# Retention and a gated FFN on one core: two batches side by side, 64 tokens at a time

## Chip, core and metric

The kernel runs on one NeuronCore of a Trainium2 chip. The metric is the time of one execution in microseconds (us) on the device. TensorE multiplies matrices into PSUM, VectorE (DVE) and ScalarE (ACT) work elementwise, GpSimd (POOL) takes a few small operations, and SyncE (SP) issues nearly all DMAs. Each engine runs its instructions in the order in which the program lists them.

## What is computed

There are 4 batches, 8 heads of width 64 and 768 tokens. The first half is a retention: per batch and head a state of 64 x 64 decays by a head's own factor and takes in one outer product per token. The second half is a feed-forward layer of width 1,024 with a convolution over three tokens inside its gate.

```python
for t in range(S):                                    # S = 768
    state = gamma * state + einsum('bhd,bhe->bhde', k[:, :, t], v[:, :, t])
    y[:, :, t] = scale * einsum('bhd,bhde->bhe', q[:, :, t], state)
x = y.transpose(0, 2, 1, 3).reshape(B, S, 512)
h = maximum(x @ w_in, 0)                              # w_in 512 x 1024
conv = sum(conv_w[k] * shifted(h, k - 1) for k in range(3))
out = (h * sigmoid(conv)) @ w_out                     # w_out 1024 x 512
```

Everything is float32. The three weight arrays arrive as 64-bit floating-point words seen as pairs of 32-bit integers, and the kernel itself makes from them float32 values, split into a high part and a low part.

## The kernel before

**Retention.** Time is cut into pieces of 64 tokens. Decay is taken out of the recurrence by scaling v with gamma^-t (`scale_v`) and the result with gamma^t (`decay`, with the table `gy_sb`). A *chunk* `n` is 128 tokens of one batch, two pieces `s`, so there are 24 chunks. For a piece, `mix(n, s)` issues three sorts of products of 64 x 64, all on line L456: the state's update (`ps_st`), the result from masked scores and from the carried state (`ps_y`), and the scores of the chunk that follows (`ps_s`). State and scores lie on the diagonal quarters of the array ("straight"), the result on the other two ("crossed"), and they are issued two and two. Before the next piece can be mixed, ScalarE copies the state from PSUM (`carry`, L484), and VectorE masks the scores (`masked`, L476) and scales v (L420; from chunk 17 on POOL does).

**From y to x.** `decay` (L489) writes a chunk's x, ScalarE copies it as high part into `xu` (`x_head`, L503), VectorE writes the rest as low part (`x_rest`, L509), and POOL copies edge columns between neighbouring units (`halo`, L519).

**Weights.** 16 pieces of 128 x 512, 8 of `w_in` and then 8 of `w_out`, are loaded and turned into float32 by one ScalarE and five VectorE operations (`w_abs` to `w_low`, L547 to L581). ScalarE writes the high half (`w_head`, L598). For the low half there are two ways: for the first `SUMMED` = 6 pieces TensorE adds up three products with unit matrices (`w_sum`, L606 to L608) and ScalarE copies the sum (`w_add`, L626); for the others VectorE subtracts and adds (`w_rest` L613, `w_add` L628). A ninth, tiny one is the convolution's weights.

**FFN.** A *unit* `u` is 256 tokens of one batch with an edge column on both sides (258 columns); there are 12. `mm1(u, f)` (L640) computes 128 of the 1,024 hidden columns in 12 matmuls (four slices of x, three products of high and low parts). It needs weight piece `f`, and the halo from the next chunk. Then come `relu` (L649), `conv_tap` (L656), two `conv_side` (L661) per `f`, and per pair `p` of them `gate` (L667), `gated` (L672), `g_head` (L677), `g_rest` (L682). `mm2(u, t, p)` (L696) is 6 matmuls of 512 columns for 128 tokens `t`, and `put` copies and stores.

**Order and buffers.** No engine chooses at run time. `list_tasks` lists all steps with an assumed duration, what they need and which buffers they take; `tensor_sequence` gives TensorE's wanted order, and `plan` places step after step by these durations, slacks (`SLACK`) and windows; the steps are emitted in the order of their planned starts. Where the plan sees TensorE wait early in the program it adds warm-up matmuls on a tile of zeros (`keep_warm`, L386). Retention buffers `rw` are three, weights and gated values share four `g`, hidden values and `w_out` share 31 `h`, and PSUM has one bank for scores, two for results, two for `mm1`, two for `mm2`.

Of the kernel before, what the change touches and what calls it, by code (L numbers as in the profile page):

```python
# [20 lines left out]
NC = S // P  # L21
# [3 lines left out]
U = NT * P  # L25
UH = U + 2
NU = S // U
N_CHUNKS, N_UNITS = B * NC, B * NU
CONV = 2 * NF
LAST = (N_UNITS - 1, NT - 1)  # L30

# [10 lines left out]
BUFS = {"rw": 3, "x": 5, "xu": 3, "g": 4, "m": 2, "es": 1, "h": 31, "cv": 3, "ps_s": 1, "ps_y": 2, "ps_m": 2, "ps_o": 2}  # L42
# [5 lines left out]
LATENCY, SAME = {DMA: 2600, PE: 250}, {DMA: 0, PE: 50}  # L48
OTHER = 60
FIRST = {PE: 4800.0, DVE: 1200.0, ACT: 2000.0, POOL: 700.0, DMA: 700.0}  # L50
WARM_UP = 8
WARM_NS = 216
# [4 lines left out]
SWITCH = 95  # L57
MIX = 950
USE = {"scores": 0.25, "mix": 0.5, "mm1": 0.98, "mm2": 0.98, "w_sum": 0.98}

ATT_FIRST, ATT_RATE = 5, 16.5

CONV_FIRST, CONV_RATE, CONV_LAG = 24, 10.5, 32
SUM_LEAD, SUM_LEAD_OUT = 14, 201
AHEAD = 10984
WINDOW = {PE: 85200, POOL: 98300, DMA: 97750, DVE: 150}
STAY = 26
PACE = 1.4

SLACK = {  # L70
    "x_rest": 38500, "halo": 23000, "w_in": 42000, "w_out": -7500, "mix": -1000, "carry": -8000,
    "masked": 6000, "make_gy": 59500, "x_head": 44500, "scores": 36000, "g_rest": 14000, "scale_v": 8500,
    "conv_w": 28500,
}

VECTOR_V, VECTOR_X, SUMMED = 17, 48, 6
# [3 lines left out]
        "g_rest", "halo"}  # L80

def has_state(n, s):
    return (n % NC, s) != (NC - 1, 1)


def list_tasks():
# [6 lines left out]
    for n in range(N_CHUNKS):  # L93
        b, c = divmod(n, NC)
        u = n // NT

        before = ("load", n - 1) if n > 1 else n and ("load_kv", 0)
        task(("load", n), DMA, 4 * P * D * H * (4 if n else 2) * BYTE, [before], take="rw")
        if n == 0:
            task(("load_kv", 0), DMA, 4 * P * D * H * 2 * BYTE, [("load", 0)])  # L100
        vector = n < VECTOR_V
        task(("scale_v", n), DVE if vector else POOL, 690 if vector else 1230, [("load", n) if n else ("load_kv", 0)])
        if n == 0:
            for s in range(2):
                task(("scores", 0, s), PE, 485, [("load", 0), s and ("scores", 0, 0)], take=None if s else "ps_s")
        task(("masked", n), DVE, 690, [("mix", n - 1, 1) if n else ("scores", 0, 1)], free="ps_s")
        for s in range(2):

            prev = (n, 0) if s else (n - 1, 1) if c else (n - 1, 0) if b else None
            after = [("scale_v", n), ("masked", n), prev and ("carry", *prev)]  # L110
            after += [("mix", n, 0) if s else n and ("mix", n - 1, 1)]
            after += [n + 1 < N_CHUNKS and ("load", n + 1)]
            take = None if s else "ps_y" if n + 1 == N_CHUNKS else ("ps_y", "ps_s")
            task(("mix", n, s), PE, MIX, after, take, "rw" if s else None)
            if has_state(n, s):
                task(("carry", n, s), ACT, 370, [("mix", n, s)])
        if n == 0:
            task(("load_gy",), DMA, 4 * P * NPAIR * P * BYTE)
        elif n < NC:
            task(("make_gy", c), ACT, 1300, [("load_gy",)])  # L120
        task(("decay", n), DVE, 690, [("mix", n, 1), ("make_gy", c) if c else ("load_gy",)], "x", "ps_y")
        if n % NT == 0:
            task(("x_tiles", u), POOL, 60, [u and ("x_tiles", u - 1)], take="xu")
        task(("x_head", n), ACT, 620, [("decay", n), ("x_tiles", u)])
        vector = n < VECTOR_X
        task(("x_rest", n), DVE if vector else POOL, 690 if vector else 1280, [("x_head", n)], free="x")
        if n % NT == NT - 1 and u % NU + 1 < NU:
            task(("halo", n, 1), POOL, 620, [("x_rest", n), ("x_tiles", u + 1)])
        if n % NT == 0 and u % NU > 0:
            task(("halo", n, -1), POOL, 620, [("x_rest", n), ("x_tiles", u - 1)])  # L130

    task(("load_eye",), DMA, 300)
    task(("eyes",), ACT, 500, [("load_eye",)])
    for i in range(CONV + 1):
        big = i < CONV
        ns = lambda t: t if big else 90
# [4 lines left out]
        task(("w_abs", i), ACT, 670 if big else 220, [("load_w", i)], take="m" if big else None)  # L141
        task(("w_clamp", i), DVE, ns(410), [("w_abs", i)])
        task(("w_shift", i), DVE, ns(410), [("w_clamp", i)])
        task(("w_sign", i), DVE, ns(680), [("w_shift", i)])
        task(("w_power", i), DVE, ns(410), [("w_sign", i)])
        task(("w_low", i), DVE, ns(680), [("w_power", i)], take="es" if big and i < SUMMED else None)
        if not big:
            task(("w_add", i), DVE, 90, [("w_low", i)])
            continue
        task(("w_head", i), ACT, 620, [("w_sign", i)], take="h" if i >= NF else None)  # L150
        if i < SUMMED:
            task(("w_sum", i), PE, 1500, [("w_head", i), ("w_low", i), ("eyes",)], take="ps_m", free=("g", "m", "es"))
            task(("w_add", i), ACT, 600, [("w_sum", i)], take="h" if i >= NF else None, free="ps_m")
        else:
            task(("w_rest", i), DVE, 690, [("w_head", i), ("w_power", i)])
            task(
                ("w_add", i), DVE, 690, [("w_low", i), ("w_rest", i)], take="h" if i >= NF else None, free=("g", "m")
            )

    for u in range(N_UNITS):  # L160
        x = [("x_tiles", u)] + [("x_rest", NT * u + t) for t in range(NT)]
        x += [u % NU and ("halo", NT * u - 1, 1), u % NU + 1 < NU and ("halo", NT * u + NT, -1)]
        for f in range(NF):
            before = (u, f - 1) if f else (u - 1, NF - 1) if u else None
            task(
                ("mm1", u, f), PE, 1452, [("w_add", f), before and ("mm1", *before)] + (x if f == 0 else []),
# [3 lines left out]
            task(("relu", u, f), ACT, 380, [("mm1", u, f)], take=None if odd else "h", free="ps_m")  # L170
            task(
                ("conv_tap", u, f), ACT, 490, [("relu", u, f), ("w_add", CONV), odd and ("conv_tap", u, f - 1)],
                take=None if odd else "cv",
            )
            task(("conv_side", u, f, 0), DVE, 450, [("conv_tap", u, f)])
            task(("conv_side", u, f, 2), DVE, 450, [("conv_side", u, f, 0)])
            if not odd:
                continue
            task(("gate", u, p), ACT, 640, [("conv_side", u, f - 1, 2), ("conv_side", u, f, 2)])
            task(("gated", u, p), DVE, 690, [("gate", u, p)], free="h")  # L180
# [3 lines left out]
                ("g_head", u, p), ACT, 630,  # L184
                [("gated", u, p), before and ("g_head", *before), u and not p and ("load_w", CONV - 1)], take="g",
            )
            task(("g_rest", u, p), DVE, 690, [("g_head", u, p)], free="cv")
        for t in range(NT):
            halves = 2 if (u, t) == LAST else 1
            for h in range(halves):  # L190
                for p in range(NF // 2):
# [4 lines left out]
                        ("mm2", u, t, p, h), PE, 1400 / halves, need,  # L196
                        take=None if p else "ps_o", free="g" if t == NT - 1 and h == halves - 1 else None,
                    )
                task(("put", u, t, h), ACT, 580 / halves, [("mm2", u, t, NF // 2 - 1, h)], free="ps_o")
# [3 lines left out]
def tensor_sequence(tasks):  # L203

    visits = [[("scores", 0, s) for s in range(2)]] + [[("mix", n, s)] for n in range(N_CHUNKS) for s in range(2)]
    parts = []
    for u in range(N_UNITS):
        for p in range(NF // 2):
            j = NF * u + 2 * p + 1
            step = max(j + CONV_LAG, CONV_FIRST + CONV_RATE * j // 10) + 5  # L210
            parts += [(step, ("mm2", u, t, p, 0)) for t in range(NT)]
    sequence, sums, done, step = [], [], 0, -1
    while step < N_UNITS * NF or parts:

        for i in range(NF) if step < 0 else ():
            late = [(i - SUM_LEAD, ("w_sum", i))] if i < SUMMED else []
            late += [(CONV_FIRST + i - SUM_LEAD_OUT, ("w_sum", NF + i))] if NF + i < SUMMED else []
            sums += late
        sums.sort()
        while sums and sums[0][0] <= step:  # L220
            sequence.append(sums.pop(0)[1])
        if 0 <= step < N_UNITS * NF:
            sequence.append(("mm1", step // NF, step % NF))
        goal = max(done, min(ATT_FIRST + int(ATT_RATE * (step + 1) / 10), len(visits)))
        sequence += [k for some in visits[done:goal] for k in some]
        done = goal
        if parts and parts[0][0] <= step:
            sequence.append(parts.pop(0)[1])
        step += 1

    sequence = [k for k in sequence if k[:3] != ("mm2", *LAST)]
    return sequence + [("mm2", *LAST, p, h) for h in range(2) for p in range(NF // 2)]

# [532 lines left out]
```

## Time and profile before

| | |
|---|---|
| median of 3 timed runs | 374.64 us (373.19 to 375.74) |
| span of the profiled execution, first to last instruction | 371.3 us; the timed median stands 3.3 us above it |
| TensorE busy | 363.0 us, 98%, clock 0.999 |
| VectorE, ScalarE, POOL busy | 255.9, 203.0 and 21.3 us |
| first `mm1`, first `mm2` | 33.39 and 140.02 us |
| moved by DMA | 40.96 MB, mean 110 GB/s |

Times inside the profile count from the span's start. A row of the timeline gives start, duration, engine, line, operation, tiles and number; what stands in brackets behind it is the idle time before and what ended it. Rows of the chain give start, duration and what ran. A duration reaches to the end of an operation's result, so consecutive operations of one engine may start closer together than their durations.

### The profile page before, as it was taken

The numbers are of one execution on the slowest core, as the hardware profiler recorded it, in microseconds if no ns is written. First come the engines' busy times: TensorE is split into PE (matmuls) and PEld (weight loads), VectorE is DVE, ScalarE is ACT, GpSimd is POOL, SyncE is SP. The second block draws the span as 40 slices with busy tenths as digits, with TensorE's granted clock in tenths as the row PEclk, the third lists the DMA queues.
The fourth block names the chain that finished last, engine by engine and source line by source line (L and its number), as shares of the span: only waits on it lengthen the run. The fifth ranks groups of instructions, "written<-read, shape, count | busy, mean of one in ns | idle before, by whom it ended". The sixth has DMA issues, their size and how long they took to land.

```text
span 371.3 us, 10906 instructions
## 1 busy us (share of the span) xinstructions
PE 363.0 (98%) x4787; PEld 317.3 (85%) x4787; DVE 255.9 (69%) x484; ACT 203.0 (55%) x444; POOL 21.3 (6%) x53
## 2 busy tenths in 40 slices
PE   8999999998999989999999999999999999999996
PEld 6768778997999978889898998999899989888886
DVE  1588688898778867687657566575655555889860
ACT  3844554765444534556456456564545545678741
POOL 1001000010001121300000002010000000000000
PEclk9999999999999999999999999999999999999999
DMA  8877687406556657301000010000100001001111
GB/s 272 324 282 293 237 284 244 163 2 201 199 181 229 224 190 266 120 4 56 2 25 34 2 56 1 30 28 2 56 2 28 30 0 59 28 29 56 58 56 56
DMA packets 10047, 40.96 MB, mean 110 GB/s; under 512 B 1264, under 2 KB 1648, under 8 KB 7056
## 3 DMA queue, kind: packets, MB, share of 16 engines
q1 hardware_dynamic: 9936, 40.20, 29.6%
q8 instruction: 37, 0.61, 0.6%
q14 instruction: 10, 0.08, 0.1%
q0 software_dynamic: 64, 0.07, 0.1%
HBM read 33.98 MB, written 6.29 MB: 108 GB/s over the span
## 4 chain that ended last, share of the span: by engine, by line
PE 93%; ACT 4%; DMA 1%; issue 1%; SPq 0%; ACTq 0%
PE ps_m L640 38%; PE ps_o L696 36%; PE ps_st L456 6%; PE ps_s L456 5%; PE ps_y L456 3%; PE ps_o L386 3%; PE ps_m L606 2%; ACT gy_sb L416 2%; DMA gy_sb<-in_gy 1%; ACT cv L656 1%; PE ps_m L607 0%; PE ps_m L608 0%; ACT L667 0%; ACT L416 0%; ACT h L649 0%
## 5 line engine op out<-in xcount | busy, mean ns | idle before, releaser
L640 PE MATMUL ps_m<-xu,wi_hi 128*128 128x258 f32 x768 | 145.6, 287 | 1.4 <-issue 1.3
L696 PE MATMUL ps_o<-h,g 128*128 128x512 f32 (+1 forms) x600 | 143.7, 386 | 0.0
L640 PEld LDWEIGHTS ps_m<-xu,wi_hi 128*128 128x128 f32 x768 | 122.4, 189 | 7.7 <-issue 0.8
L696 PEld LDWEIGHTS ps_o<-h,g 128*128 128x128 f32 x600 | 105.6, 188 | 19.7
L640 PE MATMUL ps_m<-xu,wi_lo 128*128 128x258 f32 x384 | 108.7, 283 | 0.7 <-issue 0.7
L661 DVE SCALAR_TENSOR_TENSOR cv<-h,cw_sb,cv 128x256 f32<-128x256 f32 x192 | 85.7, 481 | 17.5 <-ACT cv L656 15.8
L640 PEld LDWEIGHTS ps_m<-xu,wi_lo 128*128 128x128 f32 x384 | 72.7, 189 | 1.4 <-issue 1.4
L649 ACT ACTIVATE h<-ps_m 128x258 f32<-128x258 f32 x96 | 36.4, 379 | 54.1 <-PE ps_m L640 53.6
L456 PE MATMUL ps_y<-rw 64*64 64x64 f32 x1472 | 54.1, 221 | 0.9 <-issue 0.9
L656 ACT ACTIVATE cv<-h,cw_sb 128x256 f32<-128x256 f32 x96 | 46.4, 503 | 15.4 <-DVE g L682 15.4
L682 DVE TENSOR_TENSOR g<-cv,g 128x512 fp32r<-128x512 f32 x48 | 33.2, 692 | 27.7 <-ACT g L677 27.6
L456 PEld LDWEIGHTS ps_y<-rw 64*64 64x64 f32 x1472 | 47.1, 134 | 1.5 <-issue 1.5
L672 DVE TENSOR_TENSOR cv<-h,cv 128x512 f32<-128x512 f32 x48 | 33.1, 690 | 22.1 <-ACT cv L667 21.8
L677 ACT CAST g<-cv 128x512 fp32r<-128x512 f32 x48 | 29.8, 621 | 26.3 <-PE ps_o L696 22.6
L667 ACT ACTIVATE cv<-cv 128x512 f32<-128x512 f32 x48 | 30.2, 630 | 25.4 <-DVE cv L661 25.0
L476 DVE TENSOR_TENSOR rw<-ps_s,mask_sb 128x512 f32<-128x512 f32 x24 | 16.5, 689 | 24.1 <-PE ps_y L456 14.4
L456 PEld LDWEIGHTS ps_st<-rw 64*64 64x64 f32 x704 | 24.0, 134 | 10.5 <-issue 3.2
L456 PE MATMUL ps_s<-rw 64*64 64x64 f32 x768 | 31.1, 219 | 1.1 <-issue 1.0
L456 PE MATMUL ps_st<-rw 64*64 64x64 f32 x704 | 30.2, 224 | 0.1
L456 PEld LDWEIGHTS ps_s<-rw 64*64 64x64 f32 x768 | 26.7, 135 | 2.6 <-issue 1.5
L484 ACT COPY rw<-ps_st 128x256 f32<-128x256 f32 x44 | 16.3, 370 | 10.9 <-PE ps_st L456 10.6
L386 PE MATMUL ps_o<-o_sb 128*128 128x512 f32 x67 | 20.5, 444 | 1.1 <-DVE o_sb L380 1.1
(48 smaller groups left out, 216.0 us busy)
## 6 DMA issues: line engine op xcount, KB each, us to landing
rw<-in_qkv SPq DMA_DIRECT2D x23, 1024.0 KB, 4.9
out_y<-o_sb SPq DMA_DIRECT2D x23, 256.0 KB, 2.0
g<-in_w_in SPq DMA_DIRECT2D x8, 512.0 KB, 7.3
g<-in_w_out SPq DMA_DIRECT2D x8, 512.0 KB, 5.6
rw<-in_qkv SPq DMA_DIRECT2D x2, 512.0 KB, 5.2
gy_sb<-in_gy SPq DMA_DIRECT2D x1, 256.0 KB, 4.7
out_y<-o_sb SPq DMA_DIRECT2D x2, 128.0 KB, 1.7
eye_sb<-in_eye SPq DMA_DIRECT2D x1, 64.0 KB, 10.1
```

What stands on the lines that cost most here:

```text
L386: nc.tensor.matmul(ps, warm, warm.unsqueeze(1).broadcast_to([P, 4, P]), start=True, stop=True)
L456: nc.tensor.matmul(out, lhsT, rhs, start=start, stop=stop, skip_group_check=True)
L476: nc.vector.tensor_tensor(out=rw[n][:, 1], in0=s_ps.pop(n), in1=mask_sb.unsqueeze(1).unsqueeze(1).broadcast_to([P, 2, NPAIR, C]), op=ALU.mult,
L640: nc.tensor.matmul(h_ps[u, f][:, :UH], w[:, k, fs], x[:, k, :], start=(i == 0), stop=(i == len(products) - 1))
L649: nc.scalar.activation(hs[u, p][:, i], h_ps.pop((u, f))[:, :UH], AF.Relu)
L656: nc.scalar.activation(cvs[u, p][:, i], hs[u, p][:, i, 1 : U + 1], AF.Copy, scale=cw_sb[:, f, 1:2])
L661: nc.vector.scalar_tensor_tensor(out=cv, in0=h[:, k : k + U], scalar=cw_sb[:, f, k : k + 1], in1=cv, op0=ALU.mult, op1=ALU.add)
L667: nc.scalar.activation(cvs[u, p], cvs[u, p], AF.Sigmoid)
L672: nc.vector.tensor_tensor(out=cv, in0=hs.pop((u, p))[:, :, 1 : U + 1], in1=cv, op=ALU.mult)
L677: nc.scalar.copy(gs[u, p][:, 0], cvs[u, p])
L682: nc.vector.tensor_tensor(out=lo, in0=cvs.pop((u, p)), in1=hi.bitcast(F32), op=ALU.subtract)
L696: nc.tensor.matmul(ps, g[:, ts], w[f][:, cs], start=(f == 0 and i == 0), stop=(f == NF - 1 and i == 2))
```

## The change

A chunk is now 64 tokens of two batches (`NC = S // C`); there are again 24, 12 for each pair of batches. `mix(n)` has twice the products of a `mix(n, s)`, and the state of two batches fills a whole PSUM bank. Batches 0 and 1 go first, then 2 and 3. A unit is 128 tokens of two batches with edges on both (260 columns), fed by two chunks.

- `SUMMED = 0`: no weight sums; VectorE makes all low halves.
- `scale_v` is done by ScalarE for all chunks, four activations of 128 x 2 x 64 each, in place of one VectorE or POOL operation.
- `gy_sb` is made by three VectorE operations, not twenty of ScalarE; constants come in one load.
- The first six chunks (`ALONE`) load q, k and k, v apart, and their scores are issued on their own, not inside the mix before.
- `x_rest` stays on VectorE, `carry` copies 512 columns at a time.
- The planner has new assumed durations, slacks and rules, so the order is new on each engine.

```diff
-NC = S // P
+NC = S // C
-U = NT * P
-UH = U + 2
-NU = S // U
-N_CHUNKS, N_UNITS = B * NC, B * NU
+UH = P + 2
+NU = S // P
+N_CHUNKS, N_UNITS = B // 2 * NC, B // 2 * NU
...
-ATT_FIRST, ATT_RATE = 5, 16.5
...
+ATT_RATE, ATT_FIRST, MM2_LAG, SKEW, SKEWED = 0.62, -7.1, 30, 0, 12
...
-VECTOR_V, VECTOR_X, SUMMED = 17, 48, 6
+SCALED = {DVE: 13, ACT: 24}
+ALONE = 6
+SUMMED = 0
...
     def scale_v(n):
-        (nc.vector if n < VECTOR_V else nc.gpsimd).tensor_tensor(
-            out=rw[n][:, 3], in0=rw[n][:, 3], in1=gvf_sb[:, n % NC, :2].unsqueeze(3).broadcast_to([P, 2, NPAIR, C]),
-            op=ALU.mult,
-        )
+        v, by = rw[n][:, 3], gv[:, n % NC]
+        if scaled_by(n) == ACT:
+            for g in range(NPAIR):
+                nc.scalar.activation(v[:, :, g], v[:, :, g], AF.Copy, scale=by[:, g : g + 1])
+            return
...
+    def of_state(n):
+        pair, c = divmod(n, NC)
+        if c == 0:
+            st_ps[pair] = ps_buf("ps_st", (P, 2, NPAIR, D))
+        for b, g, j in heads:
             r = HALF[j]
...
+            yield st_ps[pair][r, b, g], rw[n][r, 2, b, g], rw[n][r, 3, b, g], first, c == NC - 2
...
+    def mix(n):
+
+        across = list(of_y(n))
+        straight = list(of_state(n)) if has_state(n) else []
+        straight += list(of_scores(n + 1)) if ALONE <= n + 1 < N_CHUNKS else []
         for i in range(0, max(len(across), len(straight)), 2):
             for product in straight[i : i + 2] + across[i : i + 2]:
                 multiply(*product)
...
-    def carry(n, s):
-
-        nc.scalar.copy(rw[n + s][:, 4, 1 - s], st_ps[n // NC])
+    def carry(n):
+
+        nc.scalar.copy(rw[n + 1][:, 4], st_ps[n // NC])
```

Below are three places of the order. A row is line, operation, output and inputs, shape and how many in a row; line numbers are those of the version it stands in.

TensorE in the version before, where the first weight sum stands between two mixes (`eye_sb`, `minus`, `plus` are unit matrices):

```order
L456 MATMUL ps_s<-rw 64x64 x2
L456 MATMUL ps_y<-rw 64x64 x2
L606 MATMUL ps_m<-m,eye_sb 128x512
L607 MATMUL ps_m<-wi_hi,minus 128x512
L608 MATMUL ps_m<-es,plus 128x512
L456 MATMUL ps_st<-rw 64x64 x2
L456 MATMUL ps_y<-rw 64x64 x2
```

TensorE in the changed version, from the end of the mix of chunk 3 over the first `mm1` to the scores of chunk 5 (`ps_o<-o_sb` is a warm-up matmul):

```order
L470 MATMUL ps_st<-rw 64x64 x2
L470 MATMUL ps_y<-rw 64x64 x18
L396 MATMUL ps_o<-o_sb 128x512
L653 MATMUL ps_m<-xu,wi_hi 128x260 x2
L653 MATMUL ps_m<-xu,wi_lo 128x260
...
L470 MATMUL ps_s<-rw 64x64 x16
```

The sums are gone from this engine. Over the whole program retention stands in 24 rows of mostly 64 matmuls in place of 49 of mostly 32, and there are 28 warm-up matmuls in place of 67.

VectorE in the version before, around the third weight piece (`es` is what a weight sum takes):

```order
L476 TENSOR_TENSOR rw<-ps_s,mask_sb 128x512
L489 TENSOR_TENSOR x<-ps_y,gy_sb 128x512
L420 TENSOR_TENSOR rw<-rw,gvf_sb 128x512
L557 TENSOR_SCALAR m<-m 128x512
L565 SCALAR_TENSOR_TENSOR m<-g,m 128x512
L573 TENSOR_SCALAR g<-m 128x512
L581 SCALAR_TENSOR_TENSOR es<-g 128x512
```

VectorE in the changed version, around the first weight piece:

```order
L578 SCALAR_TENSOR_TENSOR m<-g,m 128x512
L504 TENSOR_TENSOR x<-ps_y,gy_sb 128x512
L490 TENSOR_TENSOR rw<-ps_s,consts_sb 128x512
L586 TENSOR_SCALAR g<-m 128x512
L594 SCALAR_TENSOR_TENSOR g<-g 128x512
L524 TENSOR_TENSOR xu<-x,xu 128x8x64
L626 TENSOR_TENSOR m<-m,wi_hi 128x512
L565 TENSOR_SCALAR m<-m 128x512
L641 TENSOR_TENSOR wi_lo<-m,g 128x4x128
```

The scaling of v (L420) has left, each piece has the subtraction and the addition (L626, L641) in addition, and steps of the next piece (here L565) stand between dependent ones.

ScalarE in the version before, and then in the changed one, around the first high halves of `w_in`:

```order
L598 CAST wi_hi<-m 128x4x128
L626 CAST wi_lo<-ps_m 128x4x128
L484 COPY rw<-ps_st 128x256
L503 CAST xu<-x 128x4x128
L547 ACTIVATE m<-g 128x512
```

```order
L611 CAST wi_hi<-m 128x4x128
L560 ACTIVATE m<-g 128x512
L497 COPY rw<-ps_st 128x512
L437 ACTIVATE rw<-rw,consts_sb 128x2x64 x4
L518 CAST xu<-x 128x8x64
L663 ACTIVATE h<-ps_m 128x260
```

The copy of the sums (L626 of before) is gone, and the four scalings (L437) stand between the copy of a state and the high half of x.

More of the change, by code (lines that the diff above doesn't have):

```diff
@@ L93, in list_tasks @@
     for n in range(N_CHUNKS):
-        b, c = divmod(n, NC)
+        c = n % NC
         u = n // NT
-        before = ("load", n - 1) if n > 1 else n and ("load_kv", 0)
-        task(("load", n), DMA, 4 * P * D * H * (4 if n else 2) * BYTE, [before], take="rw")
+        half = 4 * P * D * H * 2 * BYTE
+        whole = n >= ALONE
+        before = n and ("load" if n > ALONE else "load_kv", n - 1)
+        task(("load", n), DMA, half * (1 + whole), [before], take="rw")
         if n == 0:
-            task(("load_kv", 0), DMA, 4 * P * D * H * 2 * BYTE, [("load", 0)])
@@ L101, in list_tasks @@
[L101 to L121, printed above, removed]
+            task(("load_consts",), DMA, 4 * P * N_CONSTS * BYTE, [("load", 0)])
+        if not whole:
+            task(("load_kv", n), DMA, half, [("load", n), ("load_consts",)])
+        scale = scaled_by(n)
+        task(
+            ("scale_v", n), scale, {DVE: 600, ACT: 1170, POOL: 1050}[scale],
+            [("load" if whole else "load_kv", n), ("load_consts",)],
+        )
@@ new lines, in list_tasks @@
+        if not whole:
+            task(("scores", n), PE, 940, [("load", n), n and ("masked", n - 1)], take="ps_s")
+        after = ("mix", n - 1) if whole else ("scores", n)
+        task(("masked", n), DVE, 605, [after, ("load_consts",)], free="ps_s")
+        after = [("scale_v", n), ("masked", n), n and ("mix", n - 1), c and ("carry", n - 1)]
+        after += [ALONE <= n + 1 < N_CHUNKS and ("load", n + 1)]
+        take = ("ps_y", "ps_s") if ALONE <= n + 1 < N_CHUNKS else "ps_y"
+        task(("mix", n), PE, 1900, after, take, "rw")
@@ L122, in list_tasks @@
+        if has_state(n):
+            task(("carry", n), ACT, 480, [("mix", n)])
+        if n < NC - 1 and n % GY_AT_ONCE == 0:
+            task(("make_gy", n // GY_AT_ONCE), DVE, 1140, [("load_consts",)])
+        task(("decay", n), DVE, 605, [("mix", n), c and ("make_gy", (c - 1) // GY_AT_ONCE)], "x", "ps_y")
         if n % NT == 0:
             task(("x_tiles", u), POOL, 60, [u and ("x_tiles", u - 1)], take="xu")
-        task(("x_head", n), ACT, 620, [("decay", n), ("x_tiles", u)])
-        vector = n < VECTOR_X
@@ new lines, in tensor_order @@
+def tensor_order(tasks):
+    rank = {}
+    for n in range(N_CHUNKS):
+        rank["mix", n] = ATT_FIRST + n * ATT_RATE
+        rank["scores", n] = ATT_FIRST + (n - 1) * ATT_RATE - 0.1
+    for i in range(SUMMED):
+        rank["w_sum", i] = i + (SUM_AT if i < NF else SUM_AT_OUT)
+    for u in range(N_UNITS):
+        for f in range(NF):
+            rank["mm1", u, f] = NF * u + f - min(u, SKEWED) * SKEW
+        for t in range(NT):
+            for h in range(2):
+                for p in range(NF // 2):
+                    rank["mm2", u, t, p, h] = NF * u + 2 * p + MM2_LAG + t + (500 * (h + 1) if (u, t) == LAST else 0)
+    rank = {k: v for k, v in rank.items() if k in tasks}
+    return {k: i for i, k in enumerate(sorted(rank, key=rank.get))}
```

353 lines of the change are left out of this document (169 added, 184 removed).

## The prediction

> **What bounds the kernel now.** I read the page's engine totals and forty slices first, then the chain that ended last, then the timeline of TensorE and VectorE for single durations.
>
> ```profile
> span 371.3 us, 10906 instructions
> PE 363.0 (98%) x4787; PEld 317.3 (85%) x4787; DVE 255.9 (69%) x484; ACT 203.0 (55%) x444; POOL 21.3 (6%) x53
> PE   8999999998999989999999999999999999999996
> DVE  1588688898778867687657566575655555889860
> GB/s 272 324 282 293 237 284 244 163 2 201 199 181 229 224 190 266 120 4 56 2 25 34 2 56 1 30 28 2 56 2 28 30 0 59 28 29 56 58 56 56
> PE 93%; ACT 4%; DMA 1%; issue 1%; SPq 0%; ACTq 0%
> ```
>
> TensorE is full almost from start to end and carries 93% of the chain. [...] So I price TensorE's program kind by kind, by the distance between starts.
>
> ```profile
> 209.97 1.45 PE ps_m L640 x12
> 211.41 1.40 PE ps_o L696 x6
> ...
> 232.66 1.44 PE ps_m L640 x12
> ...
> 313.59 54.49 PE ps_o L696 x258
> 368.14 0.37 ACT o_sb L705
> ```
>
> The last row of products with `w_out` is 210 matmuls of full width and 48 of half: 54.49 us over 234 is 0.2329 us, so one `mm2` (6 matmuls) takes 1.397 us. An `mm1` and an `mm2` alternate eight times from 209.97 to 232.66, 2.836 us a pair, which leaves 1.44 us for an `mm1` of 12 matmuls. Behind 368.14 lie 3.2 us of copy, store and end.
>
> ```profile
> 108.33 1.63 PE ps_m L640 x12
> 111.06 1.63 PE ps_m L640 x12
> 113.78 1.63 PE ps_m L640 x12
> ...
> 13.64 0.23 PE L456 MATMUL ps_st<-rw 64*64 64x64 f32 x2
> ...
> 14.46 0.22 PE L456 MATMUL ps_s<-rw 64*64 64x64 f32 x2
> ```
>
> Inside one `mix` the starts of 14 steps lie between 13.64 and 14.46: 0.0586 us for a step of two straight and two crossed products, 0.937 us for the 16 steps of a mix. Where `mm1` and mix alternate, a round takes 2.725 us (108.33 to 113.78 is two): 2.725 - 1.44 - 0.937 = 0.345 us go to the two changes of kind, **0.173 us a change**.
>
> ```profile
> 1.05 4.21 PE L386 MATMUL ps_o<-o_sb 128*128 128x512 f32 x9 [1.05 <-DVE o_sb L380]
> 5.35 1.15 PE L456 MATMUL ps_s<-rw 64*64 64x64 f32 x32
> 6.42 4.37 PE L386 MATMUL ps_o<-o_sb 128*128 128x512 f32 x18
> 10.72 0.27 PE L456 MATMUL ps_st<-rw 64*64 64x64 f32 x2
> ...
> 24.16 0.27 PE L456 MATMUL ps_st<-rw 64*64 64x64 f32 x2
> 25.25 1.13 PE L606 MATMUL ps_m<-m,eye_sb 128*128 128x512 f32 x2
> 26.77 0.27 PE L456 MATMUL ps_st<-rw 64*64 64x64 f32 x2
> 33.39 0.51 PE L640 MATMUL ps_m<-xu,wi_hi 128*128 128x258 f32 x2
> ```
>
> The first 9 warm-up matmuls take 4.3 us; the next 18 take 4.30 us with one change, 0.23 us each; the order of before holds 67 in all, so 58 x 0.23 = 13.3 us. From 24.16 to 26.77 stand a mix, a weight sum and two changes: 2.61 - 0.937 - 0.345 = 1.33 us for one `w_sum`.
>
> The sum of before, with 98 changes between retention and anything else in its order: start 1.05, first warm-up 4.3, other warm-up 13.3, 96 `mm1` 138.2, 96 `mm2` 134.1, retention 1,472 matmuls / 32 x 0.937 = 43.1, changes 16.9, sums 6 x 1.33 = 8.0, end 3.2: 362.2 us. So only **9.1 us of the 371.3 are bare waiting**, and 13.3 us more are warm-up put into waits. The first `mm1` starts at 33.39; up to there little but retention and filler runs.
>
> **The change part by part, on TensorE.** The matmuls of retention keep their number (1,472) and shape.
> - No weight sums: -8.0 us, certain, since all six stand in the dense row.
> - 64 matmuls in a row where 32 stood: 24 rows of retention for 49, 48 changes for 98, 8.3 us for 16.9: -8.6 us. I suppose that a change costs the same however long the row is; bounds are 0 (the cost follows the matmuls) and 8.6. I take 8.6, since the 0.0586 us inside a row shows no such cost.
> - 260 columns for 258: 1.44 us x 2/258 x 96 = +1.1 us.
> - 28 warm-up matmuls for 67: -9.0 us of filler. This is no gain by itself: it comes back as waiting unless there is less to wait for.
>
> Sum without waits: 1.05 + 4.3 + 19 x 0.23 (4.4) + 139.3 + 134.1 + 43.1 + 8.3 + 3.2 = **337.7 us**. What remains is how long TensorE waits. If it waits as long as now (9.1), the span is 346.8. If the ramp needs the same time with filler or without (9.1 + 13.3 = 22.4, of which 4.4 is counted), it is 355.7. These are the first pair of ends.
>
> **On VectorE, which feeds the ramp.** It makes the low half of each weight piece, and TensorE's `mm1` of column f waits for piece f.
>
> ```profile
> 15.94 0.42 DVE L552 TENSOR_SCALAR m<-m 128x512 f32<-128x512 f32 x1
> 41.26 0.43 DVE L557 TENSOR_SCALAR m<-m 128x512 int32<-128x512 int32 x1
> 41.73 0.69 DVE L565 SCALAR_TENSOR_TENSOR m<-g,m 128x512 int32<-128x512 int32 x1
> 54.29 0.68 DVE L613 TENSOR_TENSOR m<-m,wi_hi 128x512 f32<-128x512 f32 x1
> 54.89 0.68 DVE L489 TENSOR_TENSOR x<-ps_y,gy_sb 128x512 f32<-128x512 f32 x1
> 55.49 0.68 DVE L628 TENSOR_TENSOR wi_lo<-m,g 128x512 fp32r<-128x512 f32 x1
> 60.60 0.69 DVE L628 TENSOR_TENSOR wi_lo<-m,g 128x512 fp32r<-128x512 f32 x1
> 61.21 0.69 DVE L509 TENSOR_TENSOR xu<-x,xu 128x512 fp32r<-128x512 f32 x1
> 77.64 0.75 DVE L557 TENSOR_SCALAR m<-m 128x512 int32<-128x512 int32 x2
> 305.55 1.92 DVE L661 SCALAR_TENSOR_TENSOR cv<-h,cw_sb,cv 128x256 f32<-128x256 f32 x4 [0.58 <-ACT cv L656]
> ```
>
> From start to start a 512-wide operation takes 0.60 us (54.29, 54.89, 55.49) whatever its 0.68 us of duration; a TENSOR_SCALAR 0.335 (two in 0.75), 0.12 more where the next one needs its result (41.26 to 41.73 is 0.47); a side of the convolution 0.40 (four dependent ones end after 1.92). By before's order there stand from the first clamp to the last low half of `w_in` 43 operations of 0.60, 24 of 0.335 and 26 such delays: 37.0 us. The trace has them from 15.94 to 61.2, 45.3 us: VectorE was filled to **0.817**.
>
> After the change the same stretch has 53, 26 and 8: 31.8 + 8.7 + 1.0 = 41.5 us. The six pieces cost two operations more each, the scaling of v has left, and the new order puts other work between dependent operations. The first clamp can't be much sooner than 15.94: the same 3.7 MB lie ahead of the first weight piece and in it, and the slices move 272 and 324 GB/s. So the last low half comes at 57.4 if VectorE never waits, at 66.7 if filled to 0.817.
>
> Until a matmul can use it I allow 0.25 us (an estimate: 0.08 of it is the duration beyond the 0.60, the rest a handover), and TensorE's order has 2 `mm1` (2.9), the mix of chunk 11 (48 matmuls and two changes, 1.75) and then 19 `mm1`, 176 retention matmuls and 6 changes (33.8) up to the first `mm2`: 96.1 us at the soonest, where the work before that point is 93.0. So it waits at least 3.1 us: span 340.8. At 0.817 the first `mm2` comes at 105.4, 12.4 us of waits, **span 350.1**. In the second stretch, from the last piece of `w_in` to the first `g_rest`, VectorE's order has 44 of 0.60, 16 of 0.335, 12 of 0.40 and six small ones, 37.3 us: hidden behind TensorE when dense (94.7 against 96.1), but at 0.817 it ends at 112.4 and the span is 357.1. From there on TensorE has `mm1` and `mm2` to alternate, as before from 140 on.
>
> ```profile
> 140.02 1.60 PE ps_o L696 x6
> ```
>
> There before lost almost nothing: 57 `mm1`, 96 `mm2`, 264 retention matmuls and 19 changes are 227.2 us, and 368.14 - 140.02 is 228.1. I cost that part at no waits; the cover is the products queued behind one another, and if it were gone a late half-unit would cost up to one 1.4 us `mm2` each time.
>
> **On ScalarE and the queues.** Scaling v is now four activations a chunk.
>
> ```profile
> 7.27 5.96 ACT L416 ACTIVATE gy_sb<-gy_sb,gvf_sb 128x128 f32<-128x128 f32 x20
> 15.50:61.30 45.80, 44.50 (x1060) 34.88 (x1062) 37.33 (x69) 24.31 (x52) 2.49 (x6) 1.00 0.76 275
> ```
>
> Twenty of that width took 5.96 us, so a chunk costs 1.19 us. In the ramp ScalarE was busy 24.3 of 45.8 us; nine scalings add 10.7, six `w_add` leave (3.5): some 32 of 42 to 51 us. It is hidden as a total; what it delays is the `carry` and `x_head` behind it in the queue, by 1.19 us at worst a chunk, about 12 us over ten chunks at one end and 0 at the other. The order gives it before the state is ready, so I take nothing and keep a few us in the range. The weights and chunks needed up to chunk 11 (18.5 MB) want 319 GB/s if they are to be there by 60 us; the window shows 275 moved, the best slice 324. That alone says that 57.4 won't be reached. POOL loses its scalings of v and two small loads, and SP gets four issues more in all; a scaling that waits for its chunk's load holds up the two behind it, which is part of those few us.
>
> I take a span of 351, next to the 350.1 and midway between 346.8 and 355.7. The timed runs' median, 374.64, stands 3.3 us over the profiled span, so the forecast is **354 us**.
>
> **The rivals.**
> - *The ramp closes up* (VectorE nearly dense): 340.8 to 344 span, 344 to 347 us. For it: the order interleaves two weight pieces. Against: 319 GB/s.
> - *VectorE sets both stretches*: 357.1, so 360 us. For it: 0.817 is what the trace shows.
> - *A change of kind costs more after a longer row*: the 8.6 us stay, 363 us. Against: rows of 16 and of 32 show the same steps.
> - *The clock drops in the thin start.* The row at 1.05 shows 9 matmuls at 0.47 us, twice the 0.23 of later: the array starts slow, and before put 18 more warm-up matmuls behind the first scores where now 7 stand. If it stays slow until some 15 us of work are done, that work doubles, of which 4 us fall into waits: 351 + 11 = 362, 365 us. [...]
> - *Lockstep makes the ramp serial* (the other side): decay and mask of a chunk wait on VectorE in order for its mix, the mix stands behind two `mm1`, and these wait for a low half that VectorE makes only after the former mask. If nothing overlaps, a chunk costs VectorE's 5.2 us (41.5 / 8) plus 2.9 plus 2.2 = 10.3 us for 5.2, over nine chunks 46 us on the 340.8: 387, **390 us**. It decides from a round of 8.6 us on (30.5 us over nine). Against: before's 45.3 us for eight pieces are 5.7 us a round, with the same in-order engines.
>
> **How the numbers follow.** Forecast 0.58; ramp closed up 0.14; VectorE in both stretches 0.11; clock 0.04; costly changes 0.03; serial ramp 0.06; two of the slower ones together, about 372 us, 0.04. Within 1% (371 to 378) is about what measuring this kernel can't tell from no change. So faster 0.90, same 0.04, slower 0.06. The range takes in the floor's upper part and the clock rival: 345 to 367.
>
> **What would show it.** The first `mm1` starts at 21 to 25 us instead of 33.39, the last low half of `w_in` lands at 60 to 68, the first `mm2` runs at 100 to 110 instead of 140.02, and the rest lasts 241 us up to the last `mm2`. One chunk's retention takes 2.2 us with its changes. I'm wrong if the first `mm2` comes later than 120, if windows show a clock under 1.00 after 10 us, or if the steady pairs are longer than 2.84 us.

## The result and the profile after

The changed kernel takes 359.34 us (median of five, 357.41 to 361.33) against 373.47 us for the kernel before beside it: a ratio of **0.961** (95% interval 0.957 to 0.965). Run again beside the last experiments it took 359.67 against 373.12, 0.962 (0.957 to 0.966), and left a second profile; below I compare with the middle of the two, 0.9615 of before. The forecast was 354 us. The profiled execution is the longest of the five, 361.33 us with a span of 359.5.

The page after, lines that answer to those shown of before:

```profile
span 359.5 us, 10783 instructions
PE 345.3 (96%) x4724; PEld 311.0 (87%) x4724; DVE 250.9 (70%) x482; ACT 216.7 (60%) x490; POOL 19.8 (6%) x48
PE   8769999999999999979999999999999999999996
PEclk9996999999999999989999999999999999999999
PE 88%; DMA 4%; issue 3%; ACT 2%; DVE 1%; SPq 1%; ACTq 0%
```

TensorE has 17.7 us less to be busy with (363.0 before), but its row now has holes, in the second and third slice (9 to 27 us) and in the eighteenth, and the granted clock (PEclk, the share of full speed that TensorE is given) is low in the fourth and the eighteenth. The chain of waits says what stands there: it follows the end of the program back, and its pieces are start, length and what was running (dots stand for pieces left out).

```profile
3.09 9.19 DMA rw<-in_qkv
...
14.26 1.30 issue
...
23.76 3.73 issue
...
31.03 2.50 PE ps_m L653 x12
...
149.64 0.49 issue
...
153.83 1.83 issue
...
156.01 2.72 PE ps_m L653 x12
...
205.16 1.44 PE ps_m L653 x12
206.60 1.39 PE ps_o L710 x6
208.00 1.46 PE ps_m L653 x12
...
314.13 41.89 PE ps_o L710 x204
```

The steady pairs from 205.16 to 208.00 last 2.84 us, as before. The first `mm1` comes at 31 us, not at 21 to 25, and the chain ahead of it is loads and "issue": TensorE stands still for 1.30 and 3.73 us where nothing that the profile shows holds it, in the middle of a block of fp32 products. At 153.83 it stands for 1.83 us in the same way, between two products of one mix. Behind both, an `mm1` of 1.44 us takes 2.50 and 2.72. Windows of 2 us show why (columns: the window, its length, busy time with its count, granted clock, the busy share of the DMA engines, GB/s):

```profile
24.00:26.00 2.00, 0.00 (x0) 1.00 0.99 334
28.00:30.00 2.00, 2.00 (x51) 0.50 0.23 84
30.00:32.00 2.00, 2.00 (x12) 0.50 0.42 76
157.00:159.00 2.00, 2.00 (x10) 0.50 0.87 270
```

The clock falls to half twice, from 26.5 to 33.3 us (6.8 us, the first of them still in the pause) and from 156.2 to 159.6 (3.4 us). The pauses in the list and these two drops are the main surprise of this profile; what they are was the question of most experiments.

### The profile page after: what moved, and what is told of

It reads as the page before. It is cut to its first block, busy times and chain, and to the rows that moved or that the text cites. A ratio compares the mean times of both kernels' runs of the same rounds, so it can differ in the third digit from the quotient of the medians.

```text
span 359.5 us, 10783 instructions
## 1 busy us (share of the span) xinstructions
PE 345.3 (96%) x4724; PEld 311.0 (87%) x4724; DVE 250.9 (70%) x482; ACT 216.7 (60%) x490; POOL 19.8 (6%) x48
## 4 chain that ended last, share of the span: by engine, by line
PE 88%; DMA 4%; issue 3%; ACT 2%; DVE 1%; SPq 1%; ACTq 0%
PE ps_o L710 37%; PE ps_m L653 36%; PE ps_st L470 5%; PE ps_y L470 5%; PE ps_s L470 4%; DMA rw<-in_qkv 3%; DMA g<-in_w_out 2%; PE ps_o L396 1%; ACT cv L670 1%; ACT m L560 0%; SPq L412 0%; ACT h L663 0%; SPq L416 0%; DVE cv L675 0%; DVE rw L490 0%
## 5 line engine op out<-in xcount | busy, mean ns | idle before, releaser
L653 PE MATMUL ps_m<-xu,wi_hi 128*128 128x260 f32 x768 | 145.5, 288 | 0.8 <-issue 0.5
L653 PE MATMUL ps_m<-xu,wi_lo 128*128 128x260 f32 x384 | 109.6, 285 | 0.0
L675 DVE SCALAR_TENSOR_TENSOR cv<-h,cw_sb,cv 128x256 f32<-128x256 f32 x192 | 85.6, 481 | 16.0 <-ACT cv L670 14.5
L470 PE MATMUL ps_y<-rw 64*64 64x64 f32 x1472 | 50.8, 223 | 5.1 <-issue 5.0
L663 ACT ACTIVATE h<-ps_m 128x260 f32<-128x260 f32 x96 | 36.0, 376 | 23.2 <-PE ps_m L653 22.9
L691 ACT CAST g<-cv 128x512 fp32r<-128x512 f32 x48 | 29.7, 618 | 24.4 <-PE ps_o L710 23.5
L437 ACT ACTIVATE rw<-rw,consts_sb 128x128 f32<-128x128 f32 x96 | 30.5, 392 | 6.6 <-DMA rw<-in_qkv 6.4
L470 PE MATMUL ps_s<-rw 64*64 64x64 f32 x768 | 27.4, 220 | 3.8 <-DMA rw<-in_qkv 1.9
L470 PEld LDWEIGHTS ps_s<-rw 64*64 64x64 f32 x768 | 24.8, 136 | 5.8 <-issue 2.5
L532 POOL CAST xu<-xu 128x8 fp32r<-128x8 f32 x40 | 19.2, 498 | 180.7 <-PE ps_m L653 114.6
L470 PE MATMUL ps_st<-rw 64*64 64x64 f32 x704 | 26.1, 223 | 0.0
L490 DVE TENSOR_TENSOR rw<-ps_s,consts_sb 128x512 f32<-128x512 f32 x24 | 16.4, 685 | 9.0 <-PE ps_y L470 6.9
```

The costliest lines, as they stand in the source:

```text
L437: nc.scalar.activation(v[:, :, g], v[:, :, g], AF.Copy, scale=by[:, g : g + 1])
L470: nc.tensor.matmul(out, lhsT, rhs, start=start, stop=stop, skip_group_check=True)
L532: nc.gpsimd.tensor_copy(a[:, :, :, dst : dst + 1], t[:, :, :, src : src + 1])
L653: nc.tensor.matmul(h_ps[u, f], w[:, k, fs], x[:, k].rearrange("p b t -> p (b t)"), start=(i == 0), stop=(i == len(products) - 1),)
L663: nc.scalar.activation(hs[u, p][:, i].rearrange("p b t -> p (b t)"), h_ps.pop((u, f)), AF.Relu)
L675: nc.vector.scalar_tensor_tensor(out=cv, in0=h[:, :, k : k + P], scalar=cw_sb[:, f, k : k + 1], in1=cv, op0=ALU.mult, op1=ALU.add)
```

## The experiments

**Two parts of the sum, put back or moved.** First the weight sums, in the changed kernel's order: for six pieces `w_rest` is left out, and `w_sum` and its copy on ScalarE take the place of `w_add`.

```diff
-        if i < SUMMED:
+        if i < 6:
...
+        if k[0] == "w_rest" and k[1] < 6:
+            continue
...
+        if k[0] == "w_add" and k[1] < 6:
+            w_sum(k[1])
```

> The changed kernel, everything in its order, but the first six weight pieces are summed on TensorE again: three matmuls of 512 columns (1.33 us a piece before the change) and a ScalarE copy in place of two VectorE operations of about 0.6 us pitch each. If TensorE's queue is a price list, it is 6 x 1.33 = 8.0 us slower: about 367 us against 359. If the stretch up to the first mm2 is set by VectorE (90 to 100% busy from 50 us on), the six pieces give VectorE back 6 x 1.2 = 7.2 us there and the sums lie in waits of TensorE: 352 to 359 us, no slower.

368.14 us, ratio to before 0.988 (0.983 to 0.993). The 0.0265 between that and the changed kernel are 9.9 us: the price list (8.0) and 2 us over. The chain shows the rest (start, length):

```profile
51.24 1.06 PE ps_m L619 x2
...
52.80 0.59 ACT wi_lo L639
```

After five of the six sums `mm1` also waits for ScalarE's copy. VectorE got its time back (23.7 us busy from 27 to 70 us, 35.5 in the changed kernel), and the first `mm2` still came at 121.8 us, not 110.1: the theory that VectorE alone sets the ramp fails here.

The same part in the kernel before, with one more rule that the changed kernel also has, the order of the two ReLUs of a pair:

```diff
-VECTOR_V, VECTOR_X, SUMMED = 17, 48, 6
+VECTOR_V, VECTOR_X, SUMMED = 17, 48, 0
...
-            task(("relu", u, f), ACT, 380, [("mm1", u, f)], take=None if odd else "h", free="ps_m")
+            task(("relu", u, f), ACT, 380, [("mm1", u, f), odd and ("relu", u, f - 1)], take=None if odd else "h", free="ps_m")
```

> The kernel before with one part of the change alone: no weight sums on TensorE (and the ReLUs of a pair kept in their order), the rest planned anew by its own rules. If TensorE's queue is the price list, the six sums of 1.33 us go: 8.0 us less, about 365 us. If VectorE sets the ramp of the kernel before, its 6 x 1.2 = 7.2 us more on that row make the first mm2 later by as much and filler takes the place: 372 to 381 us.

388.5 us, ratio 1.039 (1.036 to 1.042): **14.5 us slower**, 7.5 us above the upper figure expected. The groups of filler show where the time went; the first line is the kernel before, the second this one:

```profile
L386 PE MATMUL ps_o<-o_sb 128*128 128x512 f32 x67 | 20.5, 444 | 1.1 <-DVE o_sb L380 1.1
L386 PE MATMUL ps_o<-o_sb 128*128 128x512 f32 x145 | 40.7, 419 | 2.5 <-issue 1.5 <-DVE o_sb L380 1.1
```

The planner put 78 more warm-up matmuls, 20.2 us, into a ramp that it found longer, and the first `mm2` moved from 140.0 to 150.8 us. So the 8.0 us aren't a gain of that part by itself in the old schedule. How much of the loss is the rule on the ReLUs, this run doesn't tell.

**v on VectorE.** The same order, but `scale_v` is emitted as one VectorE operation for every chunk.

```diff
-        if scaled_by(n) == ACT:
+        if False:
...
-        (nc.vector if scaled_by(n) == DVE else nc.gpsimd).tensor_tensor(out=v, in0=v, in1=by, op=ALU.mult)
+        nc.vector.tensor_tensor(out=v, in0=v, in1=by, op=ALU.mult)
```

> The changed kernel in its order, but v is scaled by VectorE for all 24 chunks (one operation of about 0.69 us, four of ScalarE's together 1.28 us before). If the ramp is VectorE's, the some 14 chunks ahead of the first mm2 add about 14 x 0.6 = 8.4 us to its row there, and the whole comes to 364 to 368 us. If TensorE alone sets the time, VectorE's row has room and it stays within 2 us of 359; if ScalarE's 1.28 us was the late one at the start, it is 1 to 3 us faster.

360.97 us, ratio 0.968 (0.965 to 0.971): about 2.4 us slower than the changed kernel, with intervals that touch, and not 5 to 9. VectorE's busy time from 27 to 70 us, in the changed kernel and in this one:

```profile
27.00:70.00 43.00, 35.50 (x67) 0.93 0.73 259
27.00:70.00 43.00, 41.99 (x78) 1.00 0.77 274
```

VectorE had 7.5 us free there and took 6.5 of them. The first `mm2` starts at 109.1 in this run, against 110.1 in the changed kernel and again in its second profile, whose clock from 27 to 70 us is 0.96. So VectorE wasn't full, and its filling of 0.83 (35.50 of 43) was no limit but a row with room in it.

**No filler.** The planned warm-up matmuls are left out.

```diff
-        if k in more:
-            keep_warm(more[k])
```

> The changed kernel without the 20 planned filler matmuls (the eight at the very start stay). As a price list their 20 x 0.23 = 4.6 us and six changes of kind (6 x 0.17 = 1.0 us) would be saved: 354 us. If they stand in waits only, as 13 us of waits ahead of the first mm1 say, nothing is saved, 359 us; and if they hold the granted clock up, the rows behind the waits run at 0.6 to 0.7 of the clock for longer and it is 1 to 4 us slower, to be seen in the granted clock from 15 to 60 us.

360.87 us, ratio 0.970 (0.965 to 0.975): 3 us slower by the ratios, with intervals that overlap. Nothing was saved, so the filler stands in waits. In its profile the clock is 0.94 up to 27 us and 0.96 from there to 70; since the changed kernel's own profiles have 0.99 and 0.93 or 1.00 and 0.96, the clock's part can't be told from that.

**The price of a change of kind.** An `mm1` directly ahead of a mix is emitted in its middle instead.

```diff
+            if i == n_steps // 2 and held:
+                emit["mm1"](*held.pop()[1:])
             for product in straight[i : i + 2] + across[i : i + 2]:
```

> The changed kernel, but where a first-layer block (mm1) stands directly ahead of a mix it is put into the middle of that mix: the same matmuls, 72 changes between fp32 and fp32r rows instead of 48. At 0.173 us for each change it is 24 x 0.173 = 4.2 us slower, about 363.5 us. If the price belongs to the start and the end of a block rather than to the change, or is hidden, it stays at 359; if a change costs more after a longer row (a rival of the prediction), halving the rows makes it less than 4 us, about 361.

369.32 us, ratio 0.990 (0.986 to 0.993): 10.5 us slower. That is more than 4.2, but not because a change costs more. Where nothing waits, the rows of the chain give its price:

```profile
171.37 1.64 PE ps_m L658 x12
173.00 0.20 PE ps_s L472 x2
173.22 0.04 PE ps_s L472 x2
```

From 171.37 to 173.22 the `mm1` and the step behind it take 1.85 us, 0.35 more than the 1.44 and 0.059 of the prediction, for two changes. So 24 more cost 4.2. The changed kernel has the same price behind a row of 64:

```profile
183.12 2.01 PE ps_y L470 x64
185.13 1.64 PE ps_m L653 x12
```

The two take 3.65 us, 0.34 more than 32 steps of 0.0586 and the 1.44. The other 6 us of the split kernel are no test of the price: a pause of 2.53 us stands at 52.12, the window from 50 to 60 us has a clock of 0.71, and around 180 us TensorE waits 2.75 us, from the end of an `mm1` at 178.44 to 181.19, because its ReLU, two casts and two taps now stand on ScalarE right ahead of the copy of the state that the mix needs.

**Is the late start the weights?** The first piece of `w_in` is loaded ahead of chunk 1, and everything planned anew.

```diff
-before = n and ("load" if n > ALONE else "load_kv", n - 1)
+before = n and ("load_w", 0) if n == 1 else n and ("load" if n > ALONE else "load_kv", n - 1)
```

> The changed kernel, but the first weight piece is loaded ahead of chunk 1, and the schedule is planned anew with that. If the late start is that piece (its arithmetic runs from 16.6 to 25.9 us here), the first mm1 comes at 22 to 26 us instead of 30.8 and VectorE's row ahead of the first mm2 is 3 to 6 us shorter: 353 to 356 us. If the pause of TensorE in the middle of the third mix and the loads of the chunks set the start, the chunks come 1.5 us later and it is 359 to 361 us.

362.31 us, ratio 0.971 (0.966 to 0.976): not faster, by the ratios 3.5 us slower and so above both figures expected. The first low half of `w_in` starts at 18.0 us on VectorE, not at 25.2, yet the first `mm1` starts only at 28.5; a pause of 2.41 us stands ahead of it, at 23.36. So the first `mm1` gained 2.3 us where its weights gained 7.2: they weren't all that was late.

**What are the pauses?** The profile's queue of instructions offers a cause:

```profile
q8 instruction: 37, 0.61, 0.7%
```

These are 37 packets of 16 KB, 0.61 MB in all. If they bring TensorE's 4,724 matmuls and 4,724 weight loads, that is 255 instructions a packet and 64 bytes an instruction. It is an estimate; the two runs of TensorE's instructions alone, further below, come to much the same, with 38 packets for 9,828 of these instructions and 41 for 10,672 (259 and 260 a packet). I reckon with 256. An fp32 product here is two matmuls and two weight loads (the profile has 2,944 of each for 1,472 products), so by this a packet holds 64 products: a block of them runs through one in about 2 us (2.09 us from the end of one pause to the next in a run below, 16.78 to 18.87). Five pauses in three runs all end 2.0 to 2.7 us after a packet seen in a window of half a microsecond (the changed kernel: packets at 13.0 to 13.5, 25.0 to 25.5 and 153.0 to 153.5, pauses over at 15.56, 27.49 and 155.66; with sums 23.0 to 23.5 and 25.61; split 22.5 to 23.0 and 25.19).

The count of instructions says it more sharply. Of the instructions that the profile has for TensorE (matmuls, weight loads and a few for semaphores), 449, 961, 5,569 and 5,825 have started before the pauses at 14.26, 23.76, 149.64 and 153.83: they lie 2, 18 and 1 times 256 apart. So the pauses stand at whole steps of the estimated packet; at 149.64 it is the middle of an `mm1`. The kernel before has six such pauses on the same grid (behind 449, 961, 1,473, 3,521, 5,569 and 5,825 instructions), from 16.57 to 136.41, 3.85 us in all.

More data beside the late mixes, four loads of 320 KB into spare tiles ahead of each:

```diff
+        if k[0] == "mix" and k[1] >= 15:
+            for i in range(4):
+                nc.sync.dma_start(spare[i % 2], w_out[(4 * k[1] + i) % NF][:, :320].bitcast(I32))
```

> The changed kernel with four extra loads of 320 KB in SP's queue ahead of each mix from the sixteenth on (nobody reads what they bring). Theory: the pauses of TensorE in the middle of a mix are waits for its own instructions, 16 KB a packet, that come late behind data: then the mixes from 150 us on get pauses of 0.5 to 3.7 us with no releaser (issue), each ending 2 to 2.5 us after an instruction packet, and the time grows by 4 to 15 us. Rival: the pauses belong to the matmuls or their operands; then TensorE's row from 150 us on is as before, within 1 us, except for waits named by the real loads of rw, which stand behind the extra ones.

379.32 us, ratio 1.014 (1.012 to 1.017), 20 us slower than the changed kernel, and no clean test. What TensorE waited for between 130 and 230 us (total, times, longest):

```profile
PE ps_s L467 <- DMA rw<-in_qkv: 11.1, 4, 5.1
PE ps_m L650 <- issue: 2.3, 1, 2.3
```

All issue together is 4.7 us against 2.3 in the changed kernel, but most of the time went to real loads queued behind the extra ones. It fits both theories, so it decides nothing.

TensorE alone tells them apart, in a kernel that leaves the computation out and runs stages, here one to a line: `dense(n)` is n blocks of 64 fp32 products, `wide(n)` n filler matmuls, `loads(n, 1)` n loads of 1 MB, and `gate` waits until these have landed.

```diff
+    wide(16); dense(10); gate()
+    loads(16, 1); dense(20); wide(30); gate()
+    wide(20); dense(4); gate()
+    loads(8, 1); wide(80); gate()
```

> Not the computation, TensorE's instructions alone, in stages: 10 mixes with no data moved, 20 mixes beside 16 loads of 1 MB (about 47 us of data at the 357 GB/s seen), then the same matmuls as wide filler beside 8 loads. Theory of late instructions: the quiet mixes run at 1.87 us each without pauses, the loud ones have pauses of 0.5 to 4 us (issue) that stop when the loads are over, and the wide filler, with few instructions for its time, runs without pauses beside the loads. Rival, that dense fp32 blocks pause by themselves: pauses in the quiet mixes too. Rival, that data slows TensorE in another way: wide filler slows as well.

Rows of the chain: quiet blocks, loaded blocks, and filler from 137.85 on.

```profile
16.78 0.21 PE ps_y L394
20.23 0.21 PE ps_y L394
...
52.15 4.10 issue
...
80.76 0.26 PE ps_y L394
...
86.96 0.26 PE ps_y L394
...
137.85 7.03 PE ps_o L398 x30
```

The expectation was wrong in one half: **dense fp32 blocks pause with no data moved too**. There, with 4 GB/s moved from 12 to 47 us, all of it on the queue of instructions, a block of 64 products takes 3.45 to 4.0 us, 1.4 to 1.9 of it pause; beside loads, with 412 GB/s moved from 52 to 90 us, 6.2 us (80.76 to 86.96) and once a pause of 4.10. Wide filler beside loads stays fully busy, in a window with 425 GB/s moved:

```profile
170.00:180.00 10.00, 10.00 (x46) 1.00 1.01 425
```

So it's either a price of each fp32 block or a rate at which instructions come. These two differ when other work stands between blocks, 6, 12 or 24 wide matmuls (`rounds(n, w)` is n times a block and w of them):

```diff
+    rounds(8, 6); gate()                  # a block, then w wide matmuls
+    loads(16, 1); rounds(10, 6); gate()
+    wide(8); rounds(4, 12); gate()
+    loads(16, 1); rounds(9, 12); gate()
+    loads(16, 1); rounds(6, 24); gate()
```

> TensorE's instructions alone, not the computation: a block of 64 fp32 products (one packet of instructions) followed by 6 wide matmuls (1.4 us), by 12 (2.8 us) or by 24 (5.7 us), in stages with no data moved and in stages beside 16 loads of 1 MB. By the periods of the run before (3.45 us a packet quiet, 6.2 us loaded): quiet with 6 wide ones a round is 3.7 us, without pauses; loaded with 6 it is held to about 6.2 us, loaded with 12 (5.1 us of work) to about 6.2 us, and loaded with 24 (7.9 us of work) there is no pause. If the pause is a price of each fp32 block, it stays in every stage at 1.4 to 1.9 us.

Rows of the chain; from the start of one group of filler to the next is a round:

```profile
18.06 1.58 PE ps_o L398 x6
21.67 1.59 PE ps_o L398 x6
...
64.65 1.36 PE ps_o L398 x5
66.01 2.76 issue
...
81.23 1.59 PE ps_o L398 x6
86.44 1.59 PE ps_o L398 x6
...
152.39 2.95 PE ps_o L398 x12
158.72 2.95 PE ps_o L398 x12
165.13 2.94 PE ps_o L398 x12
...
205.48 5.67 PE ps_o L398 x24
213.17 5.67 PE ps_o L398 x24
```

Quiet, 6 wide matmuls are nearly enough: 3.61 us a round, 4.1 at most, and one pause of 0.17. Loaded, six rounds with 6 average 6.9 us (5.2 to 10.5, with the clock at half in parts), rounds with 12 take 6.3 to 6.4 where their work is 4.97, and with 24 there are two pauses of 0.74 and 0.36 and then none. The pause at 66.01 stands between two wide matmuls, and the seven pauses from 46.96 to 84.71 are each 256 matmuls and weight loads apart. In these two runs that is a **rate, about one packet in 3.45 to 4.0 us quiet and in 6.2 us beside 412 GB/s of data**, and no price of a block.

**The kernel with its blocks apart.** If so, the late pauses must go when the same mixes stand further apart. A rule in the planner holds mix 17 + i back until an `mm1` and then takes it first; TensorE's order is as it was up to the first mix that moves:

```diff
+    apart = {("mix", 17 + i): ("mm1", *divmod(45 + 3 * i, NF)) for i in range(7)}
...
+    for k, a in apart.items():
+        tasks[k][2].append(a)
+        behind[a].append(k)
+        waits[k] += 1
...
-                    rank = place[k] - STAY * (KIND[k[0]] == last) if engine == PE else late[k]
+                    rank = -1000 if k in apart else place[k] - STAY * (KIND[k[0]] == last) if engine == PE else late[k]
```

> The changed kernel; up to the 17th mix every engine's order is as it was, but the last seven mixes, which stood one to a pair of mm1 and mm2 from 142 us on, stand one to three pairs. The matmuls, the changes of kind and the loads are the same in number. If the pauses at 149 to 156 us are TensorE waiting for its instructions (one packet of 16 KB each 3.45 us beside no data, 6.2 us beside full data), a round of a mix and three pairs lasts 10.8 us for 1.2 packets, so the 2.3 us of pauses and the drop of the clock behind them (about 2 us) go: 2 to 5 us less than the changed kernel run beside it. If the pauses come from the loads' data or from what the mixes wait for, or if the late mixes hold up the units that need them, it is equal or slower.

> The changed kernel unaltered, beside the spaced one on the same chip: 357 to 361 us, and pauses of about 2 us in all between 145 and 160 us.

357.47 us, ratio 0.958 (0.955 to 0.961), against 359.67, 0.962 (0.957 to 0.966): 2.2 us less, the low end of what was expected, and the intervals overlap. One pause was left, in an `mm1` behind mixes 15 to 17, which still stood close:

```profile
146.76 1.40 PE ps_m L658 x10
148.16 2.40 issue
150.56 0.40 PE ps_m L658 x2
```

So two more were moved:

```diff
+    apart = {("mix", 15 + i): ("mm1", *divmod(43 + 3 * i, NF)) for i in range(9)}
```

> As the spaced kernel before, but the spacing begins two mixes earlier: the last nine mixes, from 132 us of the plan on, stand one to three pairs of mm1 and mm2, none beside another. In the run with seven spaced ones a pause of 2.40 us was left behind the two mixes that stood close together, with 2 MB of loads beside them, and the clock dropped behind it. If such a pause needs two blocks of instructions within the time of a late packet, none is left after 130 us: 354 to 356.5 us, against 357.5 with seven spaced ones and 359.7 unspaced. If one mix beside its loads is enough, or if what is lost at the start decides, it stays at 357 to 360 us.

**354.86 us** (352.96 to 357.43), ratio **0.949** (0.946 to 0.952): below the changed kernel's interval, and the fastest of all. TensorE from 130 to 220 us, first and last rows of nine and their sum, and the last row of products:

```profile
130.00:140.00 10.00, 10.00 (x68) 1.00 0.00 0
...
210.00:220.00 10.00, 10.00 (x181) 1.00 0.01 2
sum 90.00, PE 90.00; mean PE 10.00
...
110.66 8.34 PE ps_o L715 x36
...
310.25 41.89 PE ps_o L715 x204
```

No pause and no drop of the clock is left there. From the first `mm2` at 110.66 to the end of the last at 352.14 it's 241.5 us; in the changed kernel it was 110.26 to 356.02, 245.8, and in its second profile 244.0, with one pause of 2.18 us and no drop. Spacing the mixes thins their loads too (at most 152 GB/s in a window of 10 us from 130 to 220, where the changed kernel has up to 245 in a slice of 9 us). This run doesn't part the two; by the two runs of TensorE alone (3.45 to 4.0 us a packet quiet, 6.2 us loaded) both bear on the same rate.

## Why the prediction came out 5 us low

- **The work, 337.7 us: right.** The changes of kind cost 0.17 us each behind rows of 64 (the changed kernel) as behind shorter ones (the split kernel), so halving them is worth the 8.6 us, and the rival of costlier changes falls. The sums are worth 9.9 us when put back here, 8.0 forecast. The steady pair is 2.84 us. The term holds for both parts together; the sums alone, in the kernel before, lost 14.5.
- **241.5 us from the first `mm2` on, without waits: right as work, wrong as time.** It took 245.8 (244.0 in the second profile). The step that failed was "I cost that part at no waits": the cover named was products queued behind one another, but TensorE also needs its instructions: a mix uses up one packet in about 2 us, and in the runs of TensorE alone one came in 3.45 to 4.0 us, beside 412 GB/s in 6.2. Pauses of 2.3 us and 1.7 us lost at half clock make 4.0 of the 4.3; with the mixes apart the 241.5 us came to the tenth. The kernel before, from which the "no waits" was read, has no such pause behind its first `mm2`, but 3.85 us of them ahead of it, within the 9.1 us of bare waiting: the `issue 1%` of its page.
- **The first `mm2` at 105.4: 4.9 us early.** The first `mm1` was expected at 21 to 25 us and came at 30.8 (26.8 in the second profile). I had priced the start by loads and VectorE's first piece. In fact the scores, mixes and filler ahead of it are 536 matmuls and as many weight loads, 4.2 packets by the estimate of 64 bytes each, while the DMA engines are busy 0.83 of the time up to 27 us and 0.99 in the long pause (24 to 26 us). To that I put down the pauses of 1.30 and 3.73 us; the half clock, from 26.5 us, begins in the second. Starting earlier helps little, though: the second profile and others of nearly the same order, with the first `mm1` at 26.8 to 28.5, still had their first `mm2` at 108 to 111. What holds the ramp in between isn't settled. Of the 0.25 us that I allowed until a matmul can use VectorE's result, no run shows the 0.17 for the handover: in the profile of before the first matmul starts at 1.05, 0.05 us after `o_sb` is written (0.83 and 0.17).
- **VectorE at 0.817 as what sets the ramp: not shown.** It was 0.83 full from 27 to 70 us, and the last low half of `w_in` came at 69.4, close to the 66.7. But with 6.5 us more work put on it there, the first `mm2` was no later, and with 11.8 us less (the sums put back) it was no sooner. The number was right for a reason that doesn't hold. The rival with VectorE in both stretches, 360 us, is as near to the result as any number given, but not by its mechanism: VectorE had room up to 70 us, and 4 us were lost behind the first `mm2`, where that rival has no wait. From 70 to 110 us VectorE was busy 38.2 of 40 us, so there it is close to its limit.
- **From span to median, 3.3 us: 1.5 too high.** In every execution since, of the kernel before too, the time stands 1.7 to 2.0 us above its own span (361.33 and 359.5). The 3.3 set a median against the span of a shorter execution (371.3 and 1.8 make 373.1, not 374.64). The median run's span was 357.5 where 351 was forecast, 6.5 us, and this error hid part of it: that was luck.
- **The clock rival came in small.** Its 11 us came from some 15 us of slow work in one start, which no run shows; in their place there were two drops with the pauses, of 6.8 and 3.4 us, in which TensorE lost 2.9 and 1.7 us. By my own list a clock under 1.00 after 10 us was to show me wrong, and on that step I was.
- **ScalarE's four activations at no cost: right within 2.5 us.** Moving them to VectorE made it slower.
- **The ramp closing up and the serial ramp** didn't come.

## What to carry to other kernels

Count instructions as well as time: here 64 small products used up 256 instructions in about 2 us, where a packet of as many came in 3.45 to 4.0 us quiet and in 6.2 beside 412 GB/s. TensorE then stood for up to 4.1 us with nothing that the profile shows to blame, and "issue" in the middle of its work is how the chain showed it. Spread such blocks between long matmuls, above all beside heavy loads; here that was worth 1.3% with no operation added or taken away. A part that saves time on a full engine is worth its price only if the schedule has nothing else to put there.

## What the runs showed of the hardware

- The queue of instructions moved packets of 16 KB, by the estimate above 256 of TensorE's instructions each: in the runs of TensorE alone one in 3.45 to 4.0 us with no data moved, and in about 6.2 us beside 412 GB/s of data. I had expected pauses beside data alone. A block of 64 fp32 products uses up one in about 2 us (2.09), and in the changed kernel and in the one before the pauses lie at whole steps of 256 instructions.
- Stretches at half clock in the changed kernel last 6.8 and 3.4 us; windows within them show 0.50, and windows of 2 us clear of them 1.00 (22 to 26 us, 34 to 36). The clock went to half after pauses of 1.83 us (changed kernel, at 153.83) and 2.40 us (first spaced kernel), but not after 2.18 us in a second profile of the changed kernel. So in these runs the length of a pause alone doesn't tell whether the clock drops; what else does wasn't shown.
